# Theta of the first two batches as fp32 products of transposed x and the decoded weight; the weight's fp16 parts made beside the second batch's mixing

## The chip, the cores and the metric

One NeuronCore of a Trainium2 chip runs the whole kernel in one launch. The metric is the device time in microseconds; less is better. Inputs, output and launch are the same in both versions. A run's "span" goes from the first to the last instruction of the profiled execution.

## What is computed

Eight batches of q, k, v (8 heads, 576 positions, head dimension 64) go through a linear attention with an RMS norm, and the result x (576 x 512 per batch) goes through two mixers. The change is in the first mixer, in the angle theta:

```python
kv = np.einsum('bhsd,bhse->bhde', k, v)
out = np.einsum('bhsd,bhde->bhse', q, kv)
rms = np.sqrt(np.mean(out * out, axis=-1, keepdims=True) + 1e-06)
x = out / rms * g_norm                      # heads side by side: x is (b, 576, 512)

theta = x @ w_theta                         # 512 x 512
zr, zi = x * np.cos(theta), x * np.sin(theta)
y = einsum('ts,bsd->btd', w_tok_r, zr) + einsum('ts,bsd->btd', w_tok_i, zi)
u = x + y
x = u + np.maximum(u @ w_ch, 0.0)
...
```

The second mixer (a token part with w_tok1 and w_tok2, a channel part with w_ch1 and w_ch2) follows. The weights arrive as float64 words.

## The kernel before

**Tiling.** A batch's 576 rows are cut into five tiles r = 0 to 4, four of 128 rows and one of 64. Products are made with fp16 pairs: a factor is written as a high part and a low part, and `mm3` (lines 99 to 105 of the kernel before) accumulates high·high, high·low and low·high in one PSUM bank. So one fp32-like product of 128x128 by 128x512 is three fp16 matmuls; one theta tile (512 deep, four blocks) is twelve.

**The units that matter here.** The program is written as generator functions, advanced in turns:

- `weight_tile` and `weight` load a weight's 128 rows (float64 words), `decode` turns them into fp32 (one ScalarE row on L148, three VectorE rows on L154 to L156), and ScalarE and VectorE write the high part (L176) and the low part (L178). For w_theta the pair is `wth`, `wtl`; g_norm and the scale of the angle are folded in as the per-partition factor `gt`.
- `kv` makes k transposed times v (`kvp`, L304) in fp32 and copies it to `kvbd` (L309, L310).
- `attend(o, r)` makes one tile of x: `po` (fp32 matmuls, L324), squares on ScalarE (L335), sums on VectorE (`ss`, L337), the power -1/2 on GpSimd (`ri`, L338 and L339), and x itself on VectorE (L342). Then x must be transposed. For batch 0 TensorE does it (`px`, L350), and `split` (L67 on ScalarE, L68 on VectorE) writes the fp16 pair `xt`. For every later batch x is cut into a pair first (`xs`, L357 on ScalarE, L359 on VectorE), a DMA transposes both parts (L360), and the residual `R` is put together from them (L363 on ScalarE, L365 on VectorE).
- `rotate(o, r)` makes theta of a tile (`pt`, twelve matmuls), reduces the angle (L393, L397), takes sine and cosine (L400 to L402), multiplies with x (`cs`, L405) and writes the pair `zh`, `zl` (L409, L412). A tile r of z feeds steps r and r+4 of the mixing. The fifth tile goes another way (`rotate_last`): theta is made transposed (sixteen products of 64 columns, 48 fp16 matmuls), its pair is `zt` (L449, L452), and a DMA transposes it into the last blocks of `zh` (L457), which the ninth step of each mixing product reads.
- `mix(o, c, dt)` is the product `py` of batch b, chunk c (256 or 320 columns), block dt: nine steps of three matmuls, 27 in all. `channel` follows with `pr`.

**What sets the order.** SBUF tiles are handed to a scheduler that orders each engine's instructions at build time, following the units and its own timing of them; at run time each engine goes through its list in that order, and a row that waits holds up what stands behind it. At the start, batch 0's front (weights of w_theta, kv, attend, rotate) runs together with the decoding of the mixing weights `wm` and then of `w_ch` (`wc`). In the block of batch 0 in the main loop, its eight mixing products run beside `attend` and `rotate` of batch 1; the block of batch 1 does the same for batch 2:

```python
        if b == 0:
            run(MIX, o, nxt, None, {
                "M00": "a0 w", "M01": "a1 w", "M02": "a2 w", "M03": "a3 w", "M10": "a4 r0 w", "M11": "r1 l w", "M12": "r2 w", "M13": "w",
            })
```

Names in the rows below are those of the code; with numbers, `py001` is batch 0, chunk 0, block 1, and `px10`, `pt10`, `x10` are batch 1, tile 0.

Of the kernel before, what the change touches and what calls it, by code (L numbers as in the profile page):

```python
# [10 lines left out]
F16 = mybir.dt.float16  # L11
F32 = mybir.dt.float32
# [7 lines left out]
P = 128  # L20
SW = 32.0
ST = 256.0
MAGIC = 1.5 * 2.0**23 * ST
RAD = float(np.nextafter(np.float32(2.0 * math.pi / ST), np.float32(0)))
HALF_PI = 0.5 * math.pi
# [3 lines left out]
def attn_mixer_kernel(  # L29
# [32 lines left out]
    def bank(name):  # L62
        return ps.tile([P, 512], F32, tag="ps", name=name)

    def split(hi, lo, src, scale):

        nc.scalar.activation(hi, src, AF.Copy, scale=scale)  # L67
        nc.vector.scalar_tensor_tensor(lo, src, scale, hi, ALU.mult, ALU.subtract)  # L68
# [30 lines left out]
    def mm3(acc, parts, first=True, last=True, **more):  # L99

        n = len(parts)
        for i, (ah, al, bh, bl) in enumerate(parts):
            nc.tensor.matmul(acc, ah, bh, start=first and i == 0, stop=False, **more)  # L103
            nc.tensor.matmul(acc, ah, bl, start=False, stop=False, **more)  # L104
            nc.tensor.matmul(acc, al, bh, start=False, stop=last and i == n - 1, **more)  # L105
# [19 lines left out]
    def pair(shape, name, pool=const):  # L125
        return pool.tile(shape, F16, name=name + "h", bufs=1), pool.tile(shape, F16, name=name + "l", bufs=1)

    wt = wth, wtl = pair([P, KD, DM], "wt")
    wm = pair([P, KM, S], "wm")
    wc = pair([P, KD, DM], "wc")  # L130
    w1 = pair([P, NR, DT], "w1")
# [47 lines left out]

    def words(w):  # L180
        return (w, 1) if w.dtype == F32 else (w.bitcast(I32), 2)

    def weight_tile(pool, w, pr, j, n, scale, name, col=0, raw=None):
        at = slice(col, col + n)
# [131 lines left out]
    def attend(o, r):  # L316

        b = o.b
        if r == 0:
            o.R = mp.tile([P, KD, S], F32, tag="R", name=f"R{b}", bufs=2)  # L320
            o.x, o.xt = {}, {}
        po = bank(f"po{b}{r}")
        for hp in range(HP):
            nc.tensor.matmul(po[:, hp * P:(hp + 1) * P], o.q[:, hp, r * P:(r + 1) * P], kvbd[:, hp, :], start=True, stop=True)  # L324
        po3 = po.rearrange("p (h d) -> p h d", d=D)
        ss = fp.tile([P, H], F32, tag="ss", name=f"ss{b}{r}", bufs=3)
        ri = fp.tile([P, H], F32, tag="ri", name=f"ri{b}{r}", bufs=3)
        xs = fp.tile([P, 2, DM], F16, tag="xs", name=f"xs{b}{r}", bufs=2) if b else None
        x = o.x[r] = fp.tile([P, DM], F32, tag="x", name=f"x{b}{r}", bufs=NR + 1)
        xt = o.xt[r] = fp.tile([P, 2, KD, P], F16, tag="xt", name=f"xt{b}{r}", bufs=NR + 1)  # L330

        x3 = x.rearrange("p (h d) -> p h d", d=D)
        place = beside(o)
        yield
        place(nc.scalar.activation(x3, po3, AF.Square, scale=D**-0.5))  # L335
        yield
        place(nc.vector.tensor_reduce(ss, x3, axis=AX.X, op=ALU.add))  # L337
        nc.gpsimd.tensor_tensor(ss, ss, eps, ALU.add)  # L338
        nc.gpsimd.tensor_tensor(ri, ss, mhalf, ALU.pow)  # L339
        yield  # L340
        yield
        place(nc.vector.tensor_tensor(x3, po3, ri.unsqueeze(2).to_broadcast([P, H, D]), ALU.mult))  # L342
        n = SR if r == NR else P
        R, by = o.R[:, :, r * P:r * P + n], SW if r == NR else gs
        if b == 0:

            yield
            px = bank(f"px{r}").rearrange("p (k t) -> p k t", k=KD)
            for kk in range(KD):
                nc.tensor.transpose(px[:, kk, :], x[:, kk * P:(kk + 1) * P], ident)  # L350
            yield
            split(xt[:, 0], xt[:, 1], px, 1.0)
            nc.scalar.activation(R, px[:, :, :n], AF.Copy, scale=by)
            return
        if b > 1:
            yield
        place(nc.scalar.activation(xs[:, 0, :], x, AF.Copy))  # L357
        yield
        place(nc.vector.tensor_tensor(xs[:, 1, :], x, xs[:, 0, :], ALU.subtract))  # L359
        place(nc.sync.dma_start_transpose(xt.rearrange("p a k t -> p (a k) t"), xs.rearrange("p a d -> p (a d)")))  # L360
        for _ in range(3 if b > 1 else 2):
            yield
        place(nc.scalar.activation(R, xt[:, 0, :, :n], AF.Copy, scale=by))  # L363
        yield
        place(nc.vector.scalar_tensor_tensor(R, xt[:, 1, :, :n], by, R, ALU.mult, ALU.add))  # L365
# [10 lines left out]
    def rotate(o, r):  # L376

        b = o.b
        if r == 0:
            prepare(o)  # L380
        zh, zl, x, xt = o.zh, o.zl, o.x[r], o.xt[r]
        if r == NR:
            yield from rotate_last(o, xt)
            return
        pt = bank(f"pt{b}{r}")
        mm3(pt, [(xt[:, 0, kk, :], xt[:, 1, kk, :], wth[:, kk, :], wtl[:, kk, :]) for kk in range(KD)])

        cs = fp.tile([P, 2, DM], F32, tag="cs", name=f"cs{b}{r}", bufs=2)
        f, sn = cs[:, 0], cs[:, 1]
        place = beside(o)  # L390
        yield
        with early(o):
            place(nc.scalar.activation(f, pt, AF.Copy, bias=MAGIC))  # L393
        if b > 1:
            yield
        with early(o):
            place(nc.vector.scalar_tensor_tensor(f, f, MAGIC, pt, ALU.subtract, ALU.subtract))  # L397
        yield
        with early(o):
            place(nc.scalar.activation(sn, f, AF.Sin, scale=-RAD))  # L400
            nc.scalar.activation(f, f, AF.Abs)
            nc.scalar.activation(f, f, AF.Sin, bias=hpi, scale=-RAD)  # L402
        yield
        with early(o):
            place(nc.vector.tensor_tensor(cs, cs, x.unsqueeze(1).to_broadcast([P, 2, DM]), ALU.mult))  # L405
        yield
        at = slice(r, r + NR + 1, NR)
        with early(o):
            place(nc.scalar.activation(zh[:, at, :], cs, AF.Copy))  # L409
        yield  # L410
        with early(o):
            place(nc.vector.tensor_tensor(zl[:, at, :], cs, zh[:, at, :], ALU.subtract))  # L412

    def rotate_last(o, xt):
# [3 lines left out]
        pt = bank(f"pt{b}{NR}")[:, :KD * SR].rearrange("p (k t) -> p k t", k=KD)  # L418
        for dt in range(KD):
            ds = slice(dt * P, (dt + 1) * P)  # L420
            mm3(pt[:, dt, :], [(wth[:, kk, ds], wtl[:, kk, ds], xt[:, 0, kk, :SR], xt[:, 1, kk, :SR]) for kk in range(KD)])
        cs = fp.tile([P, 2, DM], F32, tag="cs", name=f"cs{b}{NR}", bufs=2)
        f = cs[:, 0, :KD * SR].rearrange("p (k t) -> p k t", k=KD)
        sn = cs[:, 1, :].rearrange("p (k i t) -> p k i t", k=KD, i=2)
# [344 lines left out]
    for j in range(KD):  # L769
        if j == KD - 1:  # L770
            o = load_heads(0)
        go(weight_tile(stg, w_theta, wt, j, DM, gt, "wt"))
    load_q(o, P)
    for part in range(2):
        go(kv(o, part))
# [52 lines left out]
    for b in range(B):  # L828
# [22 lines left out]
            extra += [stash_narrow(g, m) for g in range(KH) for m in range(MH)]  # L851
            before = o
        elif b == 1:
            run(MIX[:4], o, nxt, None, {})
            run(["K00"] + TOKEN1 + ["K10"] + TOKEN2, before, None, nxt, {"T00": "n0", "T02": "n1", "T10": "n2 w", "T12": "n3"})
            run(MIX[4:6] + CHANNEL[:1], o, nxt, None, {"M10": "a4 l"})
            after = loaded[0]
# [86 lines left out]
```

## Time and profile before

| | us |
|---|---|
| median of 3 runs | 1106.73 (1104.41 to 1109.35) |
| time of the profiled execution | 1103.0 |
| span of that execution | 1101.2 |
| TensorE busy | 1066.4 (97%) |
| VectorE busy | 812.7 (74%) |
| ScalarE busy | 565.7 (51%) |
| first `pr` matmul of batch 0 starts at | 105.59 |

The profiled execution's own time lies 3.7 us under the median of the runs and 1.8 us over its span. In the profile PE is TensorE's matmuls, PEld its weight loads, DVE VectorE, ACT ScalarE, POOL GpSimd, and SPq the queue that issues most DMAs. Times of rows are microseconds from the span's start. An idle time in brackets is that of the engine just before the row, with what ended it. The end of a matmul is modelled, so how fast a stream of matmuls goes is read from start to start; the same holds for VectorE, whose rows overlap a little.

### The profile page before, as it was taken

What the parts mean: (1) busy time and instruction counts of PE and PEld (TensorE: products, weight loads), DVE (VectorE), ACT (ScalarE), POOL (GpSimd) and SP (SyncE); (2) the same over time, 40 slices, a digit from 0 to 9 for tenths busy, and PEclk for the clock granted to TensorE, in tenths of its full rate; (3) what the DMA queues carried; (4) which work ended last, traced back from release to release, by engine and by line L of the source; (5) the groups of instructions that cost most, each with busy time, mean ns of one, the idle gap of its engine ahead of it and who ended that gap; (6) DMA issues with size and microseconds to landing.
All of it is one profiled execution on the core that took longest, in us unless ns stands there. A gap on an engine that the chain in (4) does not pass through costs nothing.

```text
span 1101.2 us, 21603 instructions
## 1 busy us (share of the span) xinstructions
PE 1066.4 (97%) x8884; PEld 813.7 (74%) x8884; DVE 812.7 (74%) x1475; ACT 565.7 (51%) x966; POOL 186.7 (17%) x252
## 2 busy tenths in 40 slices
PE   4779999999999999999999999999999999999998
PEld 4466776767777678776877777777777777777776
DVE  4989868887988869877654685758586775758484
ACT  3857536556465654646431645446363645446360
POOL 2250032442814518243001000000000000000000
PEclk9989999999999999999999999999999999999999
DMA  9725675867748668472456402020201102020101
GB/s 311 263 69 144 139 193 130 227 156 186 230 107 222 172 165 242 96 175 69 102 205 202 162 23 65 11 76 2 85 3 39 50 22 66 12 76 1 44 1 44
DMA packets 146626, 126.31 MB, mean 115 GB/s; under 512 B 93216, under 2 KB 123040, under 8 KB 146528
## 3 DMA queue, kind: packets, MB, share of 16 engines
q1 hardware_dynamic: 141152, 104.49, 35.1%
q0 software_dynamic: 5376, 20.45, 5.1%
q8 instruction: 69, 1.13, 0.4%
q14 instruction: 29, 0.24, 0.1%
HBM read 74.25 MB, written 29.88 MB: 95 GB/s over the span
## 4 chain that ended last, share of the span: by engine, by line
PE 86%; DVE 7%; DMA 3%; ACT 1%; issue 1%; SPq 1%; POOL 0%; ACTq 0%; DVEq 0%
PE py L104 5%; PE py L105 5%; PE py L103 5%; PE na L103 4%; PE na L105 4%; PE pa L105 4%; PE pa L104 4%; PE pa L103 4%; PE na L104 4%; PE po L324 3%; PE pr L103 2%; PE pr L104 2%; PE pr L105 2%; PE pt L104 2%; PE nc L105 2%; PE nc L103 2%
## 5 line engine op out<-in xcount | busy, mean ns | idle before, releaser
L103 PE MATMUL py<-wmh,zh 128*128 128x256 f16 (+1 forms) x576 | 165.5, 288 | 3.9 <-DMA zh<-zt 2.4
L104 PE MATMUL py<-wml,zh 128*128 128x256 f16 (+1 forms) x576 | 165.4, 288 | 0.0
L105 PE MATMUL py<-wmh,zl 128*128 128x320 f16 (+1 forms) x512 | 146.4, 287 | 0.0
L105 PE MATMUL na<-gh,wbl 128*128 128x288 f16 x384 | 109.3, 286 | 0.0
L104 PE MATMUL pa<-o,wah 128*128 128x288 f16 x384 | 109.2, 286 | 0.0
L104 PE MATMUL na<-gl,wbh 128*128 128x288 f16 x384 | 109.1, 286 | 0.0
L103 PE MATMUL pa<-o,wah 128*128 128x288 f16 x384 | 108.4, 286 | 0.0
L105 PE MATMUL pa<-o,wal 128*128 128x288 f16 x384 | 107.8, 286 | 0.0
L103 PE MATMUL na<-gh,wbh 128*128 128x288 f16 x384 | 106.0, 286 | 0.2
L625 DVE TENSOR_TENSOR gl<-sum,gh 128x1152 f16<-128x1152 f32 x48 | 65.0, 1354 | 21.9 <-ACT gh L624 21.9
L104 PEld LDWEIGHTS <-wbh 128*128 128x128 f16 x672 | 65.7, 98 | 17.7 <-issue 1.0
L104 PEld LDWEIGHTS <-wah 128*128 128x128 f16 x672 | 65.8, 98 | 16.6
L103 PEld LDWEIGHTS <-wah 128*128 128x128 f16 x672 | 65.8, 98 | 16.6
L103 PEld LDWEIGHTS <-wbh 128*128 128x128 f16 x672 | 65.7, 98 | 16.6
L105 PEld LDWEIGHTS <-wal 128*128 128x128 f16 x672 | 65.8, 98 | 16.6
L105 PEld LDWEIGHTS <-wbl 128*128 128x128 f16 x672 | 65.7, 98 | 16.6
L105 PE MATMUL pr<-uh,wcl 128*128 128x256 f16 (+1 forms) x256 | 73.1, 286 | 0.0
L104 PE MATMUL pr<-ul,wch 128*128 128x256 f16 (+1 forms) x256 | 73.1, 286 | 0.0
L103 PE MATMUL pr<-uh,wch 128*128 128x256 f16 (+1 forms) x256 | 73.0, 286 | 0.0
L103 PEld LDWEIGHTS <-zh 128*128 128x128 f16 x576 | 56.7, 98 | 19.8 <-DMA zh<-zt 2.6
L339 POOL TENSOR_TENSOR ri<-ss,mhalf 128x8 f32<-128x8 f32 x40 | 68.8, 1720 | 2.5
L624 ACT ACTIVATE gh<-sum 128x1152 f16<-128x1152 f32 x48 | 55.5, 1156 | 25.6 <-DVE sum L672 25.6
(297 smaller groups left out, 2855.1 us busy)
## 6 DMA issues: line engine op xcount, KB each, us to landing
c<-u2d SPq DMA_DIRECT2D x32, 288.0 KB, 4.3
out<-c SPq DMA_DIRECT2D x64, 144.0 KB, 1.8
q<-in_q SPq DMA_DIRECT2D x7, 1152.0 KB, 6.5
k<-in_k SPq DMA_DIRECT2D x24, 256.0 KB, 5.6
v<-in_v SPq DMA_DIRECT2D x24, 256.0 KB, 5.7
wa_r<-in_w_ch SPq DMA_DIRECT2D x24, 256.0 KB, 4.1
wb_r<-in_w_ch SPq DMA_DIRECT2D x24, 256.0 KB, 4.4
wad<-wa POOLq DMA_DIRECT2D x24, 224.0 KB, 4.0
```

Of the source, the lines that this page charges most:

```text
L103: nc.tensor.matmul(acc, ah, bh, start=first and i == 0, stop=False, **more)
L104: nc.tensor.matmul(acc, ah, bl, start=False, stop=False, **more)
L105: nc.tensor.matmul(acc, al, bh, start=False, stop=last and i == n - 1, **more)
L324: nc.tensor.matmul(po[:, hp * P:(hp + 1) * P], o.q[:, hp, r * P:(r + 1) * P], kvbd[:, hp, :], start=True, stop=True)
L339: nc.gpsimd.tensor_tensor(ri, ss, mhalf, ALU.pow)
L624: nc.scalar.activation(h.hi[:, 3:], h.s, AF.Copy)
L625: nc.vector.tensor_tensor(h.lo[:, 3:], h.s, h.hi[:, 3:], ALU.subtract)
```

## The change

Batches 0 and 1 (`EXACT = 2`) make theta with fp32 matmuls: x is transposed on TensorE, also for batch 1; ScalarE alone writes it to SBUF as fp32 with `gt` multiplied in; and the product reads the decoded fp32 `wt`, four matmuls for a tile instead of twelve (sixteen instead of 48 for the fifth tile). The fp16 pair of w_theta, which batches 2 to 7 still use, is written later and in the place of the fp32 weight (`theta_split`: ScalarE, VectorE, ScalarE), one unit after each of the first four mixing products of batch 1. Batch 1 no longer makes `xs`, its five transposing DMAs and the second row of `R`.

```diff
@@ -20,6 +20,7 @@
 P = 128
 SW = 32.0
 ST = 256.0
+EXACT = 2
 MAGIC = 1.5 * 2.0**23 * ST
 RAD = float(np.nextafter(np.float32(2.0 * math.pi / ST), np.float32(0)))
 HALF_PI = 0.5 * math.pi
@@ -125,7 +126,8 @@
     def pair(shape, name, pool=const):
         return pool.tile(shape, F16, name=name + "h", bufs=1), pool.tile(shape, F16, name=name + "l", bufs=1)
 
-    wt = wth, wtl = pair([P, KD, DM], "wt")
+    wt = const.tile([P, KD, DM], F32, name="wt")
+    wtl, wth = (wt.bitcast(F16)[:, :, i * DM:(i + 1) * DM] for i in range(2))
     wm = pair([P, KM, S], "wm")
     wc = pair([P, KD, DM], "wc")
     w1 = pair([P, NR, DT], "w1")
@@ -179,6 +181,26 @@
 
     def words(w):
         return (w, 1) if w.dtype == F32 else (w.bitcast(I32), 2)
+
+    def theta_weight(j):
+
+        if w_theta.dtype == F32:
+            load(wt[:, j], w_theta[j * P:(j + 1) * P])
+            yield
+        else:
+            raw = stg.tile([P, S, 2], I32, tag="raw", name=f"wt{j}r")[:, :DM]
+            load(raw.rearrange("p n w -> p (n w)"), w_theta.bitcast(I32)[j * P:(j + 1) * P])
+            yield
+            yield from decode(wt[:, j], raw)
+
+    def theta_split(j):
+
+        hi = fp.tile([P, 2, DM], F16, tag="xs", name=f"wt{j}h", bufs=2)[:, 0]
+        nc.scalar.activation(hi, wt[:, j], AF.Copy, scale=gt)
+        yield
+        nc.vector.scalar_tensor_tensor(wtl[:, j], wt[:, j], gt, hi, ALU.mult, ALU.subtract)
+        yield
+        nc.scalar.activation(wth[:, j], hi, AF.Copy)
 
     def weight_tile(pool, w, pr, j, n, scale, name, col=0, raw=None):
         at = slice(col, col + n)
@@ -325,9 +347,11 @@
         po3 = po.rearrange("p (h d) -> p h d", d=D)
         ss = fp.tile([P, H], F32, tag="ss", name=f"ss{b}{r}", bufs=3)
         ri = fp.tile([P, H], F32, tag="ri", name=f"ri{b}{r}", bufs=3)
-        xs = fp.tile([P, 2, DM], F16, tag="xs", name=f"xs{b}{r}", bufs=2) if b else None
+        xs = fp.tile([P, 2, DM], F16, tag="xs", name=f"xs{b}{r}", bufs=2) if b >= EXACT else None
         x = o.x[r] = fp.tile([P, DM], F32, tag="x", name=f"x{b}{r}", bufs=NR + 1)
         xt = o.xt[r] = fp.tile([P, 2, KD, P], F16, tag="xt", name=f"xt{b}{r}", bufs=NR + 1)
+        if b < EXACT:
+            xt = o.xt[r] = xt.rearrange("p a k t -> p (a k t)").bitcast(F32).rearrange("p (k t) -> p k t", k=KD)
 
         x3 = x.rearrange("p (h d) -> p h d", d=D)
         place = beside(o)
@@ -342,14 +366,14 @@
         place(nc.vector.tensor_tensor(x3, po3, ri.unsqueeze(2).to_broadcast([P, H, D]), ALU.mult))
         n = SR if r == NR else P
         R, by = o.R[:, :, r * P:r * P + n], SW if r == NR else gs
-        if b == 0:
-
-            yield
-            px = bank(f"px{r}").rearrange("p (k t) -> p k t", k=KD)
+        if b < EXACT:
+
+            yield
+            px = bank(f"px{b}{r}").rearrange("p (k t) -> p k t", k=KD)
             for kk in range(KD):
                 nc.tensor.transpose(px[:, kk, :], x[:, kk * P:(kk + 1) * P], ident)
             yield
-            split(xt[:, 0], xt[:, 1], px, 1.0)
+            nc.scalar.activation(xt, px, AF.Copy, scale=gt)
             nc.scalar.activation(R, px[:, :, :n], AF.Copy, scale=by)
             return
         if b > 1:
@@ -383,7 +407,11 @@
             yield from rotate_last(o, xt)
             return
         pt = bank(f"pt{b}{r}")
-        mm3(pt, [(xt[:, 0, kk, :], xt[:, 1, kk, :], wth[:, kk, :], wtl[:, kk, :]) for kk in range(KD)])
+        if b < EXACT:
+            for kk in range(KD):
+                nc.tensor.matmul(pt, xt[:, kk, :], wt[:, kk, :], start=kk == 0, stop=kk == KD - 1)
+        else:
+            mm3(pt, [(xt[:, 0, kk, :], xt[:, 1, kk, :], wth[:, kk, :], wtl[:, kk, :]) for kk in range(KD)])
 
         cs = fp.tile([P, 2, DM], F32, tag="cs", name=f"cs{b}{r}", bufs=2)
         f, sn = cs[:, 0], cs[:, 1]
@@ -418,7 +446,11 @@
         pt = bank(f"pt{b}{NR}")[:, :KD * SR].rearrange("p (k t) -> p k t", k=KD)
         for dt in range(KD):
             ds = slice(dt * P, (dt + 1) * P)
-            mm3(pt[:, dt, :], [(wth[:, kk, ds], wtl[:, kk, ds], xt[:, 0, kk, :SR], xt[:, 1, kk, :SR]) for kk in range(KD)])
+            if b < EXACT:
+                for kk in range(KD):
+                    nc.tensor.matmul(pt[:, dt, :], wt[:, kk, ds], xt[:, kk, :SR], start=kk == 0, stop=kk == KD - 1)
+            else:
+                mm3(pt[:, dt, :], [(wth[:, kk, ds], wtl[:, kk, ds], xt[:, 0, kk, :SR], xt[:, 1, kk, :SR]) for kk in range(KD)])
         cs = fp.tile([P, 2, DM], F32, tag="cs", name=f"cs{b}{NR}", bufs=2)
         f = cs[:, 0, :KD * SR].rearrange("p (k t) -> p k t", k=KD)
         sn = cs[:, 1, :].rearrange("p (k i t) -> p k i t", k=KD, i=2)
@@ -769,7 +801,7 @@
     for j in range(KD):
         if j == KD - 1:
             o = load_heads(0)
-        go(weight_tile(stg, w_theta, wt, j, DM, gt, "wt"))
+        go(theta_weight(j))
     load_q(o, P)
     for part in range(2):
         go(kv(o, part))
@@ -851,7 +883,8 @@
             extra += [stash_narrow(g, m) for g in range(KH) for m in range(MH)]
             before = o
         elif b == 1:
-            run(MIX[:4], o, nxt, None, {})
+            extra[:0] = [theta_split(j) for j in range(KD)]
+            run(MIX[:4], o, nxt, None, {u: "w" for u in MIX[:4]})
             run(["K00"] + TOKEN1 + ["K10"] + TOKEN2, before, None, nxt, {"T00": "n0", "T02": "n1", "T10": "n2 w", "T12": "n3"})
             run(MIX[4:6] + CHANNEL[:1], o, nxt, None, {"M10": "a4 l"})
             after = loaded[0]
```

The scheduler puts the rows in another order, too. Three places follow.

TensorE at the first row that reads the last blocks of `zh`, which the DMA of `zt` of batch 0 writes. Before (`po14` is the last attention tile of batch 1, `py010` the first product of the second chunk):

```order
L105 MATMUL py010_854<-wmh_100,zl0_229 128x320
L324 MATMUL po14_888<-kvbd_96,q1_554 128x128 x4
L103 LDWEIGHTS zh0_228
L103 MATMUL py000_624<-wmh_100,zh0_228 128x256
...
L105 MATMUL py000_624<-wmh_100,zh0_228 128x256
...
L103 MATMUL py001_674<-wmh_100,zh0_228 128x256
...
L103 MATMUL py010_854<-wmh_100,zh0_228 128x320
```

Now, where the third and fourth MATMUL rows are the first and the last of the three that make the ninth step of `py000`:

```order
L106 MATMUL py001_591<-wmh_99,zl0_216 128x256
...
L105 MATMUL py001_591<-wml_100,zh0_215 128x256
...
L104 MATMUL py000_542<-wmh_99,zh0_215 128x256
...
L106 MATMUL py000_542<-wmh_99,zh0_215 128x256
L106 LDWEIGHTS zl0_216
L106 MATMUL py001_591<-wmh_99,zl0_216 128x256
```

Before, that step of `py000` to `py003` and `py010` stands behind all the other steps of these five products and behind all five `po` of batch 1. Now only `py000` has its other steps ahead of it; behind it stand 10 matmuls of `py001`, 16 of `py002`, all 27 of `py003` and of each product of the second chunk, two `po`, four `px` and three `pt` of batch 1, up to the first `pr`.

VectorE up to `zt` of batch 0 (`zt0`). Before:

```order
L444 SCALAR_TENSOR_TENSOR cs04_513<-R0_218,cs04_513 128x4x64
L156 SCALAR_TENSOR_TENSOR wc0_1v_723<-wc0_1r_724,wc0_1v_723 128x512
L342 TENSOR_TENSOR x13_834<-po13_826,ri13_832 128x512
L178 SCALAR_TENSOR_TENSOR wcl_103<-wc0_1v_723,wch_102 128x512
L452 TENSOR_TENSOR zt0_514<-cs04_513,zt0_514 128x512
L359 TENSOR_TENSOR xs10_662<-x10_663,xs10_662 128x512
```

Now:

```order
L476 SCALAR_TENSOR_TENSOR cs04_431<-R0_205,cs04_431 128x4x64
L180 SCALAR_TENSOR_TENSOR wcl_102<-wc0_0v_584,wch_101 128x512
L366 TENSOR_TENSOR x10_580<-po10_573,ri10_579 128x512
L180 SCALAR_TENSOR_TENSOR wcl_102<-wc0_1v_638,wch_101 128x512
L440 TENSOR_TENSOR zl0_216<-cs03_396,zh0_215 128x2x512
L158 SCALAR_TENSOR_TENSOR wc0_2v_699<-wc0_2r_700,wc0_2v_699 128x512
L484 TENSOR_TENSOR zt0_432<-cs04_431,zt0_432 128x512
```

Between the first `wm` row and `zt0` the list loses the five low parts of `xt` (L68), two of the sums and three of the x rows of batch 1, and gains the three decoding rows of `wc0_2`. `x10`, which `px10` waits for, stands four rows ahead of `zt0`; `zl0` of the fourth tile two rows.

TensorE at the fifth theta tile of batch 0 and the k, v products of batch 1. Before, after the first of the 48 matmuls of `pt04`, the three products whose end lets the next k and v be loaded:

```order
L105 MATMUL pt03_433<-wth_98,xt03_296 128x512
L103 LDWEIGHTS wth_98
L103 MATMUL pt04_464<-xt04_328,wth_98 128x64
L304 MATMUL kvp1_565<-v10_544,k10_542 64x64 x8
L304 MATMUL kvp1_565<-v11_548,k11_546 64x64 x8
L304 MATMUL kvp1_565<-v12_552,k12_550 64x64 x8
```

Now, behind the whole fifth tile:

```order
L374 MATMUL px04_371<-ident_78,x04_312 128x128 x4
L412 MATMUL pt03_391<-wt_98,xt03_283 128x512 x4
L451 MATMUL pt04_414<-xt04_313,wt_98 128x64 x16
L326 MATMUL kvp1_483<-v10_462,k10_460 64x64 x8
L326 MATMUL kvp1_483<-v11_466,k11_464 64x64 x8
```

They have moved behind 16 fp32 matmuls, and the loads of the remaining k and v of batch 1, and of `wc` behind them on SP's queue, follow them.

## Rows read from the trace of the kernel before

**Rows 1.** The page, parts 1 and 2: busy time; granted clock in 40 slices
```profile
PE 1066.4 (97%) x8884; PEld 813.7 (74%) x8884; DVE 812.7 (74%) x1475; ACT 565.7 (51%) x966; POOL 186.7 (17%) x252
...
PEclk9989999999999999999999999999999999999999
```

**Rows 2.** Waits of PE, 26 to 105 us: total, times, longest
```profile
PE px L350 <- DVE x L342: 5.9, 4, 2.0
PE py L103 <- DMA zh<-zt: 2.4, 1, 2.4
PE kvp L304 <- DMA v<-in_v: 2.1, 2, 1.4
PE po L324 <- DVE x L342: 1.9, 1, 1.9
PE py L103 <- ACT zh L409: 1.5, 1, 1.5
```

**Rows 3.** Waits of PE from 105 us to the end: the largest of three
```profile
PE pu L105 <- DVE hl L72: 0.8, 2, 0.5
```

**Rows 4.** Stretches: length, busy PE, PEld, DVE, ACT, POOL; PEclk, DMA share, GB/s
```profile
62.00:72.00 10.00, 6.62 (x43) 5.20 (x42) 10.00 (x15) 5.55 (x9) 9.48 (x6) 0.83 0.00 0
83.42:87.47 4.05, 4.05 (x19) 2.36 (x19) 2.78 (x6) 2.84 (x5) 0.00 (x0) 0.58 0.99 209
87.47:105.59 18.12, 18.12 (x115) 11.15 (x114) 17.85 (x33) 13.65 (x27) 2.06 (x2) 1.00 0.59 163
```

**Rows 5.** Timeline of DVE and PE about zt: start, us, row, idle before
```profile
78.08 0.69 DVE L342 TENSOR_TENSOR x<-po,ri 128x512 f32<-128x512 f32 x1 [1.80 <-POOL ri L339]
...
79.29 0.68 DVE L452 TENSOR_TENSOR zt<-cs,zt 128x512 f16<-128x512 f32 x1
...
83.42 0.28 PE L103 MATMUL py<-wmh,zh 128*128 128x256 f16 x1 [2.38 <-DMA zh<-zt]
```

**Rows 6.** Timeline of PE, six places: starts from which steps are read
```profile
26.28 0.66 PE L350 MATMUL px<-ident,x 128*128 128x128 f32 x4 [0.56 <-DVE x L342]
26.77 1.06 PE L324 MATMUL po<-kvbd,q 128*128 128x128 f32 x8
...
48.66 0.19 PE L105 MATMUL pt<-xt,wtl 128*128 128x64 f16 x1
...
49.97 0.19 PE L105 MATMUL pt<-xt,wtl 128*128 128x64 f16 x1
...
88.12 0.38 PE L103 MATMUL pt<-wth,xt 128*128 128x512 f16 x1
...
89.41 0.30 PE L103 MATMUL py<-wmh,zh 128*128 128x320 f16 x1
...
104.64 0.30 PE L105 MATMUL py<-wmh,zl 128*128 128x320 f16 x1
...
105.59 0.27 PE L103 MATMUL pr<-uh,wch 128*128 128x256 f16 x1
105.70 0.27 PE L104 MATMUL pr<-ul,wch 128*128 128x256 f16 x1
```

**Rows 7.** Matmuls that write po after 160 us: ns least, median, most; first and last start
```profile
L324 PE MATMUL po<-kvbd,q x200: 272/275/275, 201.5 to 499.2; 128*128 128x128 f32 x100
```

**Rows 8.** Timeline of DVE, 30.7 to 33.4 us
```profile
32.06 0.67 DVE L342 TENSOR_TENSOR x<-po,ri 128x512 f32<-128x512 f32 x1
32.66 0.74 DVE L155 SCALAR_TENSOR_TENSOR wm_2v<-wmr,wm_2v 128x576 int32<-128x576 int32 x1
33.33 0.68 DVE L68 SCALAR_TENSOR_TENSOR xt<-px,xt 128x512 f16<-128x512 f32 x1
```

**Rows 9.** ScalarE's row of w_theta's last fp16 part: ns least, median, most
```profile
L176 ACT ACTIVATE wth<-wt_3v,gt x1: 712/712/712, 22.2 to 22.2; 128x512 f16<-128x512 f32 x1
```

**Rows 10.** Timeline of SP and PE: a k load of batch 1, its last k, v product
```profile
47.47 0.33 SPq L272 DMA_DIRECT2D k<-in_k  x1
...
53.19 1.06 PE L304 MATMUL kvp<-v,k 96*64 96x64 f32 x16 [0.68 <-DMA v<-in_v]
```

## The prediction, made before the changed kernel ran

> **What bounds the kernel now.** The page comes first: PE is busy for 97% of the span, and its granted clock is at 90% or more in every slice but the third [rows 1]. So the end moves only if TensorE gets other work, or waits less. Where it waits is the next view. From 26 to 105 us five of its waits sum to 5.9 + 2.4 + 2.1 + 1.9 + 1.5 = 13.8 us [rows 2]; after 105 us the largest is 0.8 us in sum [rows 3]. Behind the start, then, a microsecond more of matmuls is a microsecond more at the end, and the start is all there is to gain. The windows say who sets the pace there: from 62 to 72 us DVE is busy for 10.00 of 10 us and PE for 6.62. From 83.42 us PE no longer idles. It runs 4.05 us at a granted clock of 0.58, near the lower level, 1.2 GHz, and then 18.12 of 18.12 us at full clock, with DVE at 17.85 beside it [rows 4]. The row at 83.42 is the last wait of the start: the ninth step of the mixing, which wants `zt` transposed. DVE ends `zt` about 79.9 us, and 3.5 us later PE runs [rows 5].
>
> So the start is a race of two lists: VectorE's up to `zt`, and TensorE's behind it. I take the first `pr` matmul, at 105.59 us [rows 6], as the mark at which both versions have done the same work but for the last two theta tiles of batch 1.
>
> **What a matmul costs, old and new.** Steps from start to start at full clock [rows 6]: 256 columns fp16 0.11 us (105.59 to 105.70), 320 columns 0.136 (seven from 104.64 to 105.59), 512 columns 0.215 (six from 88.12 to 89.41), 64 columns 0.029 (45 from 48.66 to 49.97). So a theta tile costs 12 x 0.215 = 2.59 us, and the fifth 48 x 0.029 = 1.4 us. Four transposes take 0.49 us (26.28 to 26.77). No fp32 matmul of 512 columns is in the trace; the nearest is `po`, fp32 with 128 columns. Each has two records of 0.275 us [rows 7], and eight of them end after 1.06 us [rows 6], so one starts each (1.06 - 0.275) / 7 = 0.112 us, as an fp16 matmul of 256 columns does. A record then takes two fp16 passes over its columns, and a product two records: 4 x 0.215 = 0.86 us with 512 columns, **3.45 us a tile, 0.86 more than now**. This is the value I take, the row being the same kind of product. The low bound is a rival, below. For the fifth tile (32 records of 64 columns) the bounds are 0.055 us a record, if only columns count, and 0.112, if a record can't be shorter than `po`'s: 1.8 to 3.6 us, 0.4 to 2.2 more than now. I take the middle, 1.2 more, having no row nearer to either.
>
> **VectorE's list up to `zt`.** It steps 0.60 us for a row of 512 (32.06 to 32.66) and 0.67 for one of 576 [rows 8], and is dense. Up to `zt` it loses five L68, two sums and three x rows, 10 x 0.60 = 6.0 us, and gains three decoding rows of `wc`, about 1.5: 4.5 us less. The wait of 1.80 us for `ri` [rows 5] stood at an x row that is now behind `zt`; it goes, or another takes its place. So `zt` ends at 79.9 - 4.5 = 75.4, less 0 to 1.8: 73.6 to 75.4. I take 74.5, and with the 3.5 us of the DMA the ninth step may start at **78.0** (77.1 to 78.9) instead of 83.42. That is the gain: 5.4 us.
>
> **TensorE's list behind it.** Here the order costs more than that. Before, 22.2 us stood between that step and the mark. Now it comes while three of the first chunk's products are unfinished, and up to the mark stand: 56 matmuls of 256 columns, 6.15 us; four products of 27 with 320 columns, 14.7; two `po`, 1.8; four `px`, 2.0; three theta tiles, 10.3: **34.9 us**. Some of this PE could have done while it waited, but it works its list in order. Nor does it come much too early: `px10` wants `x10`, some 3 us ahead of the end of `zt` on VectorE, so about 71.5 us, and between it and the ninth step stand 4.9 us at full clock, up to 1.7 more if it starts at a clock like that of 83.42 [rows 4], which puts PE there between 76.4 and 78.1. So the mark comes at 78.0 + 34.9 = 112.9 us, 7.3 later.
>
> **Behind the mark** TensorE is the bound, and gets the fourth tile (0.86 more) and the fifth (1.2 more): 2.1 us. **The sum is 7.3 + 2.1 = 9.4 us.**
>
> **Parts at no cost.** The four extra tiles' share of batch 0 (3.4 us of PE) lies where PE waits for DVE, as does the first low part on VectorE (0.6 us, before it is dense). Batch 1 no longer needs its xs, R and five transposing DMAs: some 6 us of VectorE after `zt`, worth nothing while PE has 34.9 us to do. If PE were not the cover, it would count, as in the rival on the faster side. The late split of w_theta is eight ScalarE rows of about 0.7 us [rows 9] and four of VectorE of 0.6 [rows 8], beside batch 1's mixing; its reader is batch 2's first theta tile, a whole chunk of work later. Ahead of it on VectorE stands batch 1's `zt`; behind it wait two R rows of `py`, whose banks PE does not need at once. If that cover failed, 2.4 us of VectorE would show as a PE wait at `py`.
>
> **Against the two totals.** The profiled execution took 1103.0 us, so the sum gives 1112.4. The median of the runs shown is 1106.7, 3.7 above it; on that base I predict **1116.1 us**. The forecast's own range is 77.1 to 78.9 for the step, 0.4 to 2.2 for the fifth tile, and 1.7 for the clock: +7.6 to +13, 1113 to 1120.
>
> **The rivals.**
>
> *A product at half the price.* The step of 0.112 us in `po` could be that of loading its fp32 weights, 128 columns wide, and not of its columns. Then a record of 512 columns would take 0.215 and a tile 1.73 us, less than now: 1.72 less for each of three tiles ahead of the mark and one behind, 6.9 us off the sum, +2.5 or 1109.2: no change. The Trainium skill, page "Perfetto Trace Analysis", section "Engine Utilization", halves TensorE's peak output rate for FP32_LOW_HIGH, which would be this case if it meant the whole product. Against it, `po`'s records last as long as a matmul of 256 fp16 columns, but their ends are modelled. The page "FP8 and Floating Point Precision" of the Trainium skill, section "TensorE Precision Notes", gives a true fp32 product four passes, a rule against this change, and by it the sum stays as above. Chance 0.12.
>
> *TensorE becomes the bound of the whole start (faster).* If VectorE's relief let PE work without the waits of rows 2, 13.8 us would go, and about 3.4 us lost to the low clock (0.17 of 10 us and 0.42 of 4.05 [rows 4]), against 7 x 0.86 + 1.2 + five `px` 2.45 = 9.7 us of new work ahead of the mark and 2.1 behind: 5.4 us faster, 1101.3. What decides is when `zt` lands: under 105.6 - 34.9 - 2.1 = 68.6 us the change gains. For it speaks that VectorE gives up rows; against it, that 4.5 us take it from 83.4 to 77 at best. Chance 0.07.
>
> *The loads of k and v come late (slower still).* Their buffers come free with `kvp` of batch 1. The k load went out at 47.47 us and its product ended 6.7 us later, at 54.2 [rows 10]. Now `kvp` stands behind four dearer tiles (3.4 us) and the whole fifth (1.8 to 3.6), less about a microsecond by which the first tile starts earlier: 4 to 6 us later, 58 to 60. VectorE's list comes to its copy to `kvbd` about 59, ScalarE holds back the next z behind its own; each microsecond there delays `zt` and `x10` alike. Price 0 to 3 us, with 2 the time is 1118.1. Chance 0.15.
>
> **How the numbers follow.** About 0.5%, 5.5 us, is what a measurement of this kernel can tell from no change. Forecast 0.58, half price 0.12, TensorE-bound start 0.07, late loads 0.15; 0.08 for small errors that end near no change. Slower by over 0.5% is the late loads and all but 0.04 of the forecast, 0.69; faster 0.07 and 0.01 of the rest, 0.08; the same 0.23. The range takes in half price with a little for the spread of runs, and the late loads: 1107.5 to 1120.5. Outside lie the faster case and the outer parts of these two.
>
> **What would show it.** Right: `pt` tiles of eight records that take 3.4 us; VectorE ending `zt` between 73.5 and 75.5; the ninth step of `py000` near 78; the first `pr` near 113; from there on no new wait. A `pt` tile under 2 us is the half price; `zt` landing before 69 would make the prediction wrong on its side; a `kvp` wait of PE past 58 us, with VectorE idle at `kvbd`, is the late loads. The step that bears most is the order: were the 34.9 us behind the ninth step partly done in front of it, the sum would fall by as much.

## The result, and the profile after

The changed kernel takes 1113.84 us (median of 6 runs, 1112.70 to 1115.41), the kernel before 1106.61 beside it: a ratio of 1.0066 [1.0052, 1.0079], 7.2 us slower. A second measurement gave 1113.28, 1.0052 [1.0040, 1.0064]. The forecast of 1116.1 lies 2.3 us above. The profiled execution of the changed kernel took 1113.4 us, close to its median, that of before 3.7 us less than its own; so the profiles differ by 10.4 us in span and the medians by 7.2.

The page of the changed kernel, parts 1 and 2, answers to [rows 1]:

```profile
PE 1078.1 (97%) x8840; PEld 821.6 (74%) x8840; DVE 806.8 (73%) x1460; ACT 568.9 (51%) x970; POOL 183.1 (16%) x252
...
PEclk9979999999999999999999999999999999999999
```

Waits of PE in the changed kernel, first from 26 to 112 us, then the larger two behind it; they answer to [rows 2, 3]:

```profile
PE py L104 <- ACT zh L437: 5.4, 2, 4.3
PE px L374 <- DVE x L366: 4.6, 5, 1.2
PE kvp L326 <- DMA v<-in_v: 3.8, 2, 3.0
...
PE ph L567 <- DMA xt<-xs: 1.0, 1, 1.0
PE po L346 <- DVE kvbd L332: 0.2, 1, 0.2
```

The three rows of the start sum to 13.8 us, as the five largest of the kernel before do, and those behind it to under 1.5 us. The wait for `zt` is gone. In its place stands one of 4.3 us for `zh`, the high part of z.

The stretch from 60 us on, before and then after (length, busy PE, granted clock, DMA share, GB/s):

```profile
60.00:87.50 27.50, 21.75 (x156) 0.87 0.23 47
87.50:1100.00 1012.50, 1007.94 (x8391) 1.00 0.39 106
```

```profile
60.00:87.50 27.50, 21.50 (x155) 0.78 0.36 115
87.50:1100.00 1012.50, 1010.84 (x8337) 1.00 0.37 104
```

Behind 87.5 us TensorE is full in both, or nearly (it idles 4.6 us there before, 1.7 after). From 60 to 87.5 us the changed kernel idles as long as before and runs at a lower clock, though it has more to do.

TensorE's timeline in the changed kernel, which answers to [rows 5, 6, 10]:

```profile
31.61 3.60 PE L412 MATMUL pt<-wt,xt 128*128 128x512 f32 x8
36.82 7.03 PE L412 MATMUL pt<-wt,xt 128*128 128x512 f32 x16
43.69 0.60 PE L374 MATMUL px<-ident,x 128*128 128x128 f32 x4
...
47.56 3.68 PE L451 MATMUL pt<-xt,wt 128*128 128x64 f32 x32
51.17 1.62 PE L326 MATMUL kvp<-v,k 128*64 128x64 f32 x48
...
56.23 1.12 PE L326 MATMUL kvp<-v,k 96*64 96x64 f32 x16 [3.01 <-DMA v<-in_v]
58.71 1.12 PE L326 MATMUL kvp<-v,k 96*64 96x64 f32 x16 [0.82 <-DMA v<-in_v]
...
70.80 0.40 PE L104 MATMUL py<-wmh,zh 128*128 128x256 f16 x1 [4.30 <-ACT zh L437]
...
72.46 1.12 PE L374 MATMUL px<-ident,x 128*128 128x128 f32 x4 [0.62 <-DVE x L366]
...
78.65 0.27 PE L104 MATMUL py<-wmh,zh 128*128 128x256 f16 x1
...
113.27 0.27 PE L104 MATMUL pr<-uh,wch 128*128 128x256 f16 x1
```

Two tiles, sixteen records, run from 36.82 to 43.69, where the next `px` starts: 3.43 us a tile, four passes over its columns. The fifth tile takes 3.61 us (47.56 to 51.17), 0.113 a record. New on TensorE are thus 8 x 0.84, 2 x 2.2 and five `px` of 0.49 (72.46 is the first): some 13.6 us by these steps, 8.0 of them batch 1's. The row of 78.65 is the ninth step of `py000`. The mark, the first `pr`, moved from 105.59 to 113.27, by 7.7 us.

VectorE's timeline about z of the fourth tile, and ScalarE's row that writes its high part:

```profile
61.23 1.23 DVE L440 TENSOR_TENSOR zl<-cs,zh 128x1024 f16<-128x1024 f32 x1 [0.52 <-ACT zh L437]
62.37 0.42 DVE L156 TENSOR_SCALAR wc_0v<-wc_0v 128x512 int32<-128x512 int32 x1
...
67.16 0.42 DVE L156 TENSOR_SCALAR wc_2v<-wc_2v 128x512 int32<-128x512 int32 x1
...
68.44 1.21 DVE L433 TENSOR_TENSOR cs<-cs,x 128x1024 f32<-128x1024 f32 x1
...
71.72 0.68 DVE L366 TENSOR_TENSOR x<-po,ri 128x512 f32<-128x512 f32 x1
...
72.92 1.21 DVE L440 TENSOR_TENSOR zl<-cs,zh 128x1024 f16<-128x1024 f32 x1
...
74.66 0.68 DVE L484 TENSOR_TENSOR zt<-cs,zt 128x512 f16<-128x512 f32 x1
```

```profile
69.69 1.06 ACT L437 ACTIVATE zh<-cs 128x1024 f16<-128x1024 f32 x1 [0.50 <-DVE cs L433]
```

Between the low part of the third tile (61.23) and that of the fourth (72.92) stand ten rows that decode and split `w_ch`: seven of 0.6 us and three of 0.34, 5.2 of 11.7 us. In the kernel before, only three rows of `w_ch` stand ahead of the fourth tile's low part. Seven of the ten, 3.4 us, stand ahead of `cs` of 68.44, behind which ScalarE writes the fourth tile's `zh` at 69.69, and PE starts at 70.80. Nine stand ahead of `x10` (71.72). For `x10` PE waits once more, 0.62 us at `px10` (72.46), and its full stretch begins there.

### The profile page after: what moved, and what is told of

Read it like the earlier page. It is cut to its first block, busy times and chain, and to the rows that moved or that the text cites. A ratio compares the mean times of both kernels' runs of the same rounds, so it can differ in the third digit from the quotient of the medians.

```text
span 1111.6 us, 21488 instructions
## 1 busy us (share of the span) xinstructions
PE 1078.1 (97%) x8840; PEld 821.6 (74%) x8840; DVE 806.8 (73%) x1460; ACT 568.9 (51%) x970; POOL 183.1 (16%) x252
## 3 DMA queue, kind: packets, MB, share of 16 engines
q1 hardware_dynamic: 135872, 103.18, 33.4%
## 4 chain that ended last, share of the span: by engine, by line
PE 83%; DMA 6%; DVE 6%; ACT 2%; SPq 2%; issue 1%; POOL 0%; DVEq 0%; ACTq 0%
PE py L106 5%; PE py L104 5%; PE py L105 5%; PE na L104 4%; PE na L106 4%; PE na L105 4%; PE pa L106 4%; PE pa L105 4%; PE pa L104 4%; PE po L346 3%; PE pt L412 2%; PE nc L104 2%; PE nc L106 2%; PE nc L105 2%; PE pc L106 2%; PE pc L105 2%
## 5 line engine op out<-in xcount | busy, mean ns | idle before, releaser
L104 PE MATMUL py<-wmh,zh 128*128 128x320 f16 (+1 forms) x576 | 166.0, 289 | 5.4 <-ACT zh L437 5.4
L105 PE MATMUL py<-wml,zh 128*128 128x320 f16 (+1 forms) x576 | 166.1, 289 | 0.0
L104 PEld LDWEIGHTS <-zh 128*128 128x128 f16 x576 | 56.8, 99 | 21.8 <-ACT zh L437 6.0
L105 PEld LDWEIGHTS <-zh 128*128 128x128 f16 x576 | 56.8, 99 | 16.1 <-issue 0.7
```

## The experiments

A letter for a theory holds within its own expectation. All ratios are to the kernel before, run beside them. First the changed kernel again.

> The changed kernel once more, beside the next three on one chip. Either theory: 1.006 to 1.007 of the kernel before, as at first.

Its result is given above: 1.0052 [1.0040, 1.0064].

**Which batch's products cost?** In `e1_batch0` only batch 0 makes fp32 products, and w_theta is split in the start and no longer beside batch 1's mixing:

```diff
-EXACT = 2
+EXACT = 1
@@ behind kv of batch 1
+    for j in range(KD):
+        go(theta_split(j))
@@ block of batch 1
-            extra[:0] = [theta_split(j) for j in range(KD)]
-            run(MIX[:4], o, nxt, None, {u: "w" for u in MIX[:4]})
+            run(MIX[:4], o, nxt, None, {})
```

> Batch 0 alone in fp32; the fp16 parts of w_theta are made right after its tiles, and batch 1 goes as before (pairs, transposing DMAs). Theory W (work): TensorE is the bound from about 71 us on, so the change costs what it adds to TensorE behind that point, which is batch 1's share: five px 2.45, four tiles 3.4, the fifth tile 2.2, together 8.1 us; batch 0's share lies in TensorE's waits. Then this run is at 1113.8 - 8.1 = 1105.7 us, 1104 to 1108. Theory O (order and late loads): the loss is the waits of TensorE between 52 and 71 us, made by the products of k and v behind the fifth tile; these stand there in this kernel too, so it stays above 1110 us.

1107.12 us, 0.9990 [0.9975, 1.0006]: no change. Batch 0's 5.6 us of new TensorE work cost nothing there in sum; the first `pr` starts at 106.93, 1.3 us later than before. Batch 1 transposes by DMA again, and PE waits for it (PE's timeline):

```profile
86.11 0.39 PE L104 MATMUL pt<-wt,xt 128*128 128x512 f16 x1 [2.14 <-DMA xt<-xs]
94.40 0.39 PE L104 MATMUL pt<-wt,xt 128*128 128x512 f16 x1 [1.86 <-DMA xt<-xs]
```

`e2_transpose` takes a part of the rest: the kernel before, with x of batch 1 transposed on TensorE and split into fp16 parts as batch 0's is, without fp32 products.

```diff
-        xs = fp.tile([P, 2, DM], F16, tag="xs", name=f"xs{b}{r}", bufs=2) if b else None
+        xs = fp.tile([P, 2, DM], F16, tag="xs", name=f"xs{b}{r}", bufs=2) if b > 1 else None
@@ further down in attend
-        if b == 0:
+        if b < 2:
             px = bank(f"px{b}{r}")
```

> The kernel before, with only batch 1's transposes moved to TensorE (px, low part by VectorE from PSUM); all products stay fp16 pairs. Theory W: five px, 2.45 us of TensorE, are the whole price: 1106.6 + 2.5 = 1109 us, 1107.5 to 1110. Theory O: the list of TensorE stays near that of before, k and v are loaded as before, so no loss or a small gain from VectorE's relief: 1104 to 1107 us.

1108.49 us, 1.0006 [0.9997, 1.0015]: no change. The time lies in the range of theory W, the ratio (1107.3 on the 1106.6 that the expectation starts from) between the two. Neither part alone makes the loss; batch 1's fp32 products without batch 0's were not run. `e4_three` gives a third batch the fp32 products (`EXACT = 3`, the split one batch later):

> The changed kernel with batch 2 in fp32 as well (the fp16 parts of w_theta are made at the start of batch 2's mixing). Batch 2's transposes and products lie where TensorE has next to no waits. Theory W: the price of one more batch, 8.1 us, once more: 1121.9 us, 1120.5 to 1123.5. Theory O: no more waits at the start, so 1113.8 to 1116 us.

1125.47 us, 1.0153 [1.0139, 1.0167], 9.6 to 11.2 us more than the changed kernel (1.0153 less its 1.0052 to 1.0066) and above both expectations: 8 us of TensorE work, and new PE waits for x and for transposes (behind 116 us 2.7 us in sum for x, and 2.2 for transposes where the changed kernel has 1.0).

**Does the same work cost the same in both batches?** Theta of two tiles is made twice, 6.9 us of PE with no result added, in batch 1 (`e10_twice1`), in batch 0 (`e9_twice0`), and in batch 0 with the k, v products moved as below (`e11_kv_twice0`):

```diff
-            for kk in range(KD):
+            for i in range(2 * KD if b == 1 and r < 2 else KD):
+                kk = i % KD
```

> The changed kernel with theta of batch 1's first two tiles made twice: eight more fp32 products, 2 x 3.43 = 6.9 us of TensorE, with no result added; all else and its order as it was. Theory D (batch 1's products stand where TensorE is dense): the whole 6.9 us show, 1113.6 + 6.9 = 1120.5, ratio near 1.012. Rival H (they lie beside work of other engines, and the loss comes from the order alone): under 3 us show, ratio 1.006 to 1.009.

> The changed kernel with theta of batch 0's first two tiles made twice, the same 6.9 us of TensorE. Theory F (batch 0's products lie in the start's waits, which sum to 13.8 us): 0 to 3 us show, 1113.6 to 1116.6, ratio 1.006 to 1.009. Rival L (there the products hold back the k, v products and the z behind them, so the start has no slack left): 4 to 7 us show, ratio 1.009 to 1.012.

> The same doubling of batch 0's first two tiles, on the version with the k, v products of batch 1 ahead of the fifth theta tile (1110.5, ratio 1.0028). By F 0 to 3 us show, 1110.5 to 1113.5. If only the late k and v made the doubling dear in the other run, this one shows 3 us less of it than that one; if TensorE's list is the bound of the start by itself, 5 to 7 us, 1115.5 to 1117.5, ratio 1.007 to 1.009.

Batch 1: 1120.67 us, 1.0119 [1.0097, 1.0141], 6.8 to 7.4 us over the changed kernel's two medians. Batch 0: 1115.22 us, 1.0072 [1.0054, 1.0089], under 2 us over it. With k, v first: 1109.78 us, 1.0027 [1.0018, 1.0036], against 1.0028 without the doubling: nothing. So what is added in batch 0 is free or nearly so and what is added in batch 1 is paid in full, as the timeline of `e10_twice1` shows: sixteen records without an idle time ahead of them.

```profile
91.16 7.03 PE L413 MATMUL pt<-wt,xt 128*128 128x512 f32 x16
102.13 7.03 PE L413 MATMUL pt<-wt,xt 128*128 128x512 f32 x16
```

The two runs in batch 0 are less clean than the one in batch 1: with the doubled rows the scheduler put VectorE's list in another order (in `e9_twice0` nine rows of `w_ch` stand ahead of `zt`, eleven in the changed kernel), while `e10_twice1` keeps its order but for a few neighbours. And the first `pr` does come later in both, by 1.9 us in `e9_twice0` (115.13) and by 1.1 us in `e11_kv_twice0` (110.26 for 109.12).

**Do the late loads of k and v cost?** `e3_kv_first` puts the k, v products of batch 1 ahead of the fifth theta tile of batch 0:

```diff
     for r in range(NR + 1):
+        if r == NR:
+            nxt = load_heads(1)
+            for part in range(2):
+                go(kv(nxt, part))
         go(rotate(o, r))
@@ behind the loop
-    nxt = load_heads(1)
-    for part in range(2):
-        go(kv(nxt, part))
```

> The changed kernel with the k, v products of batch 1 ahead of the fifth theta tile of batch 0, so that the late loads go out some 3.6 us earlier. Theory W: the waits for k and v (3.0 and 0.8 us) shrink, zt and x10 come up to 1.5 us earlier: 1112.3 to 1113.8 us. Theory O: the waits were the loss, the time falls by 3 us or more, to 1110.8 or under.

1110.52 us, 1.0028 [1.0018, 1.0039]: 2.7 to 4.2 us of the loss are gone, and the mark comes at 109.12; by its range theory O holds. Rows of PE, ACT and DVE:

```profile
66.85 0.40 PE L104 MATMUL py<-wmh,zh 128*128 128x256 f16 x1 [3.40 <-ACT zh L437]
```

```profile
65.75 1.04 ACT L437 ACTIVATE zh<-cs 128x1024 f16<-128x1024 f32 x1
```

```profile
60.05 1.22 DVE L440 TENSOR_TENSOR zl<-cs,zh 128x1024 f16<-128x1024 f32 x1
...
67.11 1.22 DVE L440 TENSOR_TENSOR zl<-cs,zh 128x1024 f16<-128x1024 f32 x1
68.24 0.69 DVE L484 TENSOR_TENSOR zt<-cs,zt 128x512 f16<-128x512 f32 x1
...
75.12 0.43 DVE L156 TENSOR_SCALAR wc_0v<-wc_0v 128x512 int32<-128x512 int32 x1 [1.17 <-ACT wc_0v L150]
```

`zt` starts 6.4 us earlier, the mark only 4.15, about as the row of 70.80 does (66.85). So it is z of the fourth tile, not `zt`, that releases PE here; for `x10`, right behind it, PE no longer waits. I first read this run as the price of the late loads. But the third tile's z gained only 1.2 us (60.05 for 61.23); the other 5.2 come with `w_ch`'s rows, all of which the scheduler had moved behind `zt` as well (the first starts at 75.12). The run mixes two causes.

The same move was made in `e1_batch0` (`e6_batch0_kv`) and in the kernel before (`e7_before_kv`), and in the changed kernel the attention of batch 1 was, beside it, put two mixing products later (`e8_attend_later`, `"M00": "w", "M01": "w", "M02": "a0 w"` and so on).

> Batch 0 alone in fp32, and the k, v products of batch 1 ahead of its fifth theta tile: the two edits that each gave time back. Theory S (two separate losses: late loads about 4 us, batch 1's work on TensorE the rest): both come back, 4 us under the run with batch 0 alone, 0.9955 to 0.997 of the kernel before. Rival C (one cover for both): with batch 0 alone TensorE waits 4.0 us for the transposing DMAs of batch 1 later on, so earlier loads only lengthen those waits: 0.998 to 1.001.

> The kernel before with the k, v products of batch 1 put ahead of the fifth theta tile in the program. Theory S: its list has them there but for one matmul, so nothing changes: 0.999 to 1.001. Rival: the early place is a gain of its own, not the cure of a loss that the change made: 0.996 or under.

> The changed kernel with the k, v products early, and batch 1's attention and theta units started two mixing products later, so that more mixing steps stand ahead of the wait for the fourth tile of z (3.4 us in the run with early k, v alone, which came to 1.0028). Theory F (that wait can be filled with ready steps): 2 to 3 us less, 1.000 to 1.001. Theory L (TensorE's work is the same and batch 1's chain only starts later): no gain, 1.0025 to 1.005.

`e6_batch0_kv`: 1107.82 us, 0.9999 [0.9989, 1.0008], as its rival C said. Its mark is at 102.58, 3.0 us ahead of the kernel before, and nothing is left of that at the end: behind the mark PE waits 2.2 us for v of batch 2 and 1.5 for `zt` of batch 1. `e7_before_kv`: 1105.15 us, 0.9982 [0.9971, 0.9992], some 2 us faster, between its two expectations; here, too, `w_ch`'s rows moved behind `zt` (76.55, the first of them 83.56). `e8_attend_later`: 1112.36 us, 1.0041 [1.0029, 1.0052], no better than `e3_kv_first`, as its theory L said.

**Or is it the decoding of `w_ch`?** `e12_wc_later` is the changed kernel, k and v where they were, with the decoding started five mixing products later:

```diff
-                "M00": "a0 w", "M01": "a1 w", "M02": "a2 w", "M03": "a3 w", "M10": "a4 r0 w", "M11": "r1 l w", "M12": "r2 w", "M13": "w",
+                "M00": "a0", "M01": "a1", "M02": "a2", "M03": "a3", "M10": "a4 r0", "M11": "r1 l w w", "M12": "r2 w w", "M13": "",
```

> The changed kernel with k and v of batch 1 where the change has them, but the decoding of w_ch started five mixing products later, so that its loads stand behind the transpose of zt on SP's queue and its rows behind zt on VectorE's list, as they came to stand in the version with the k, v products first. Theory W (what that version gained came from w_ch's rows leaving VectorE's list ahead of the fourth tile's z): the wait of TensorE for v and of ScalarE for kvp stay near 3.8 and 4.1 us, zt still ends some 5 us earlier, near 70, and the time falls to 1109.5 to 1111.5, ratio 1.003 to 1.0045. Theory K (it came from the early k and v): zt moves by less than 2 us and the time stays within 1 us of 1113.5, ratio 1.0055 to 1.0065. If zt lands early and the time stays, the decoding of w_ch has become a new wait ahead of the first pr, which the trace would show as PE waiting at pr.

1105.69 us, 0.9987 [0.9978, 0.9995]: the whole loss is gone, twice what was expected. Its DVE timeline, a row of ACT, a row of PE, PE's waits from 26 to 116 us, and the stretches from 60 us on:

```profile
61.28 1.23 DVE L440 TENSOR_TENSOR zl<-cs,zh 128x1024 f16<-128x1024 f32 x1 [0.52 <-ACT zh L437]
...
68.52 1.22 DVE L440 TENSOR_TENSOR zl<-cs,zh 128x1024 f16<-128x1024 f32 x1
69.65 0.69 DVE L484 TENSOR_TENSOR zt<-cs,zt 128x512 f16<-128x512 f32 x1
```

```profile
67.36 1.05 ACT L437 ACTIVATE zh<-cs 128x1024 f16<-128x1024 f32 x1
```

```profile
70.18 0.27 PE L104 MATMUL py<-wmh,zh 128*128 128x256 f16 x1
```

```profile
PE px L374 <- DVE x L366: 4.0, 4, 1.2
PE kvp L326 <- DMA v<-in_v: 2.9, 2, 2.6
PE py L104 <- ACT zh L437: 1.1, 1, 1.1
```

```profile
60.00:87.50 27.50, 26.41 (x190) 0.88 0.24 62
87.50:1100.00 1012.50, 1010.96 (x8360) 1.00 0.38 106
```

k and v are nearly as late as ever (PE waits 2.9 us for v, the third tile's z comes at 61.28, as in the changed kernel), so the loss can go without earlier loads; what earlier loads would add to this version was not tried. z of the fourth tile comes earlier, its high part by 2.3 us (67.36 for 69.69) and its low part by 4.4, and the wait of 4.3 us for it is gone. TensorE also finds more to do meanwhile: the first nine matmuls of the third and of the fourth mixing product now stand ahead of it on PE's list, where the changed kernel has the third product behind `px10` and the rest further back. With them, a `po` and `px10` done, PE comes to the row that reads this z at 70.18, only 0.6 us earlier than in the changed kernel. From 60 to 87.5 us PE is busy 4.9 us longer, at a clock of 0.88 for 0.78, which as an estimate is worth 2.75 us of 27.5: 7.7 us, about the difference between the two versions (7.2 in span, 8 in median).

The rows of `w_ch` and the order of PE's list changed together in this run, and neither was changed alone. `e3_kv_first` bears on the split. There, too, no row of `w_ch` stands ahead of `zt`, k and v come earlier, and z of the fourth tile comes earlier than here (`zh` at 65.75), yet PE waits 3.4 us for it and the time is 4.8 us longer. So a VectorE list clear of `w_ch`, with earlier k and v beside it, gave 2.7 to 4.2 us there; the rest of the 8 us went with something that only `e12_wc_later` has, and what its trace shows is the order of PE's list, with ready work ahead of the wait. That this order is the cause is argued from the traces and not shown by a run. The same edit on the kernel before was not tried; in `e7_before_kv`, where `w_ch`'s rows moved behind `zt` together with the earlier k and v, both were worth some 2 us.

## Why the prediction was right, and what it missed

Time without TensorE's work, as an estimate from each profile: idle is the span less PE's busy time, and what the clock cost is the span times its shortfall from 1.

| | span | idle | lost to the clock | both |
|---|---|---|---|---|
| before | 1101.2 | 34.8 | 6.6 (0.994) | 41.4 |
| after | 1111.6 | 33.5 | 8.9 (0.992) | 42.4 |
| `e10_twice1` | 1119.0 | 31.8 | 9.0 (0.992) | 40.8 |
| `e3_kv_first` | 1108.5 | 30.1 | 6.7 (0.994) | 36.8 |
| `e11_kv_twice0` | 1108.4 | 27.2 | 2.2 (0.998) | 29.4 |
| `e12_wc_later` | 1104.4 | 28.5 | 5.5 (0.995) | 34.0 |

The change added 11.7 us to TensorE's busy time (13.6 by the steps above) and took nothing from what it loses. `e12_wc_later` has the same products and loses 8.4 us less.

- **TensorE bounds the end: right.** Doubled products of batch 1 appear in full.
- **The price of a product: right.** 3.43 us a tile for 3.45, so half price falls. The Trainium skill's four passes for a true fp32 product (page "FP8 and Floating Point Precision", section "TensorE Precision Notes") agree with this row; the halved rate of the Trainium skill's page "Perfetto Trace Analysis" (section "Engine Utilization"), read as that of a whole product, does not. **The fifth tile was mis-sized**: it takes the upper bound, 2.2 us more and not 1.2, since a record of 64 columns is no shorter than one of 128.
- **VectorE's list: right in size.** `zt` ended at 75.3 (73.6 to 75.4 was forecast, 74.5 taken).
- **The ninth step: the number right, the reason wrong, and in part luck.** It starts at 78.65 for 78.0, but waits for nothing. The step that failed is that this row starts when `zt` lands. The DMA of `zt` goes out at 75.36 and takes 3.2 us, so it landed near 78.6, about 0.1 us before PE came (in the profile of `after_again` 1.2 us before: 73.8 + 3.2 for 78.19):

```profile
75.36 1.36 SPq L489 DMA_TRANSPOSE zh<-zt  x1
...
DMA to landing us min/median/max: 3.2/3.2/3.2
```

  What set the time is PE's own list: it stood 4.3 us for z of the fourth tile until 70.80 and 0.62 us for `x10` until 72.46, and it came out of these waits at the lower clock (0.50 granted from 70.8 to 75.5 us, 0.98 from there to 78.65). The forecast had looked at `px10` as the check on this, put PE at the ninth step between 76.4 and 78.1 by it, and passed over the z just ahead of it.
- **34.9 us behind it: right.** 113.27 - 78.65 = 34.6, so the mark was 113.27 for 112.9.
- **Behind the mark: +2.7 on the profiles for +2.1**, the fifth tile again (its 2.2 and the fourth tile's 0.84 would make 3.0). In sum +10.4 on the profiles for +9.4, but +7.2 on the medians. The error that remains, 1116.1 for 1113.84, is that of the base: the forecast carried the 3.7 us between the median and the profiled execution of before over to the changed kernel, whose profiled execution lay at its median.
- **Parts at no cost: right in the main.** Batch 0's tiles are free or nearly so (two of them doubled cost under 2 us, and nothing with k, v first); the late split of w_theta shows in no PE wait behind the mark.
- **The late loads: seen, and not needed for the loss.** The last `kvp` ended at 59.8 us (58 to 60 in that rival), and ScalarE held back the third z for 3 us behind its copy to `kvbd`:

```profile
59.87 0.38 ACT L331 ACTIVATE kvbd<-kvp 64x256 f32<-64x256 f32 x1 [4.13 <-PE kvp L326]
60.15 1.04 ACT L437 ACTIVATE zh<-cs 128x1024 f16<-128x1024 f32 x1
```

  But `e12_wc_later` keeps most of this (ScalarE waits 3.2 us for `kvp` there, 4.1 here) and has no loss.
- **The faster rival** asked for `zt` to land before 68.6 us. That point was wrong: in `e12_wc_later` VectorE only starts `zt` at 69.65, and the loss is gone all the same, since the work in front of the wait changed with it. The forecast had said that the sum would fall if the 34.9 us were partly done in front; that is what happened (32.3 us from the ninth step, 74.23, to the mark, 106.54).

So the forecast priced the given order rightly and did not see why it is dear. Two of the three rows of `w_ch` that it counted as an addition of 1.5 us are among the ten ahead of z of the fourth tile, the third stands between that z and `zt`. The scheduler used the room on VectorE for `w_ch`, and TensorE's list had too little ready work ahead of the wait, so its new work went behind the start instead of into it. How much is due to each is open.

Two versions are faster than both kernels by a little: `e7_before_kv` (0.9982) and `e12_wc_later` (0.9987). Both differences are below the 0.5% set for telling a change of this kernel from none, though their intervals exclude 1.

## What to carry to other kernels

Where one engine is full from some point on, the time is that point plus the work behind it: before pricing new work, find the one row that releases the full stretch, and see whose rows stand ahead of it on the releasing engine's list. Making a piece of work twice, in two places, tells cheaply where there is room and where there is none, as far as the order of the lists stays. And when a move helps, look for what the scheduler moved with it: here a second experiment, which kept the first one's supposed cause, showed that the loss goes without it, and the two side by side showed that the rows which both had moved explain only a part of the gain.

## What the runs showed of the hardware that was not expected

An fp32 product with 64 columns costs as much as one with 128: 0.113 us a record (32 records in 3.61 us), against `po`'s 0.112 with 128 [rows 6, 7]. As three fp16 matmuls the product of 64 columns took 0.087 us in all, as fp32 0.226.

Work that produces nothing seems to have been free not only because it lay in waits. `e11_kv_twice0` runs 6.9 us of doubled products more than `e3_kv_first` in the same time. Its stretches from 26 to 60 us and on to 87.5, and then those of `e3_kv_first`:

```profile
26.00:60.00 34.00, 30.67 (x176) 1.00 0.60 216
60.00:87.50 27.50, 23.89 (x202) 0.94 0.41 135
```

```profile
26.00:60.00 34.00, 28.66 (x194) 0.93 0.71 249
60.00:87.50 27.50, 24.10 (x177) 0.84 0.29 87
```

PE is busier by only 2.0 us in the first stretch; the granted clock is higher in both, which as an estimate is worth 0.07 x 34 + 0.10 x 27.5 = 5.1 us. The two together come near the 6.9. The rest is the mark, which comes 1.1 us later and is made up behind it, where PE's waits sum to 0.8 us for 2.2. The order of the lists differs between the two runs as well, so how much the clock alone gave back is not shown.
